# Loads, folds and copies at the head of a linear-attention and GeGLU block, in another order

## The chip, the cores and the metric

The kernel runs on one core of one Trainium2 chip. The metric is the device time of one execution in microseconds (us). A core has TensorE (matrix products, PE in the profile), VectorE (DVE), ScalarE (ACT), GpSimd (POOL) and SyncE (SP, which here issues nearly all transfers), each with its own queue of instructions. They wait for each other by semaphores. PSUM, where products land, is used here as four buffers of two banks each, handed out by a pool.

## The reference

All inputs are bf16. S = 2048 rows, D = 640, 32 heads of 20, F = 1536.

```python
n = layernorm(x)                                 # no scale, no shift
q, k, v = split_heads(n @ wqkv)                  # 32 heads of 20
pq, pk = q @ w_phi[h], k @ w_phi[h]              # 20 x 20 per head
phi(p) = concat(softmax(p), softmax(-p))
kv = einsum("bhsf,bhsd->bhfd", phi(pk), v);  z = sum over s of phi(pk)
o = (phi(pq) @ kv) / (phi(pq) . z + 1e-6)
h = x + o @ wo
out = h + (gelu(layernorm(h) @ w_gate) * (layernorm(h) @ w_up)) @ w_down
```

## The kernel before

The rows are cut into 16 tiles of 128. x lies in four groups of four tiles (`x_sb[0]` to `x_sb[3]`). A tile's LayerNorm is turned by 128 x 128 transposes into `LN1T`, whose five blocks of 128 columns ("chunks" c = 0 to 4) are the left operands of the products with W_v and with W_k. A tile's `v` is ten products of 320 columns (five chunks, two halves), and so is its `k`.

W_k isn't used as it is. It is loaded transposed (`WkT`, five loads d = 0 to 4, line 203) and multiplied with `BD`, a block matrix of w_phi and a mask (lines 430 to 434). That is `fold`: for each d six products into a PSUM buffer `wa`, and then a cast of it into `Wk2` (lines 244 to 259), by VectorE for d = 2 and by ScalarE for the others. `k` products of chunk c need fold c's cast. The exponentials of `k` are made by ScalarE straight from PSUM (line 340).

The order of the work is written out by hand: the kernel's text is the order of each engine's queue. What matters here is the head, lines 187 to 509.

- **Loads** (lines 189 to 205), issued one after another on SP: x tile 0, tile 1, tile 2, W_v chunks 0-1, chunks 2-3, x tile 3, W_v chunk 4, x tiles 4-5, then the five transposing loads of W_k. An x tile or a W_v chunk is 160 KB. x tiles 6-7 come later (line 470). The small w_phi load is on ScalarE's queue. Each load has one of eight semaphores in turn, so the ninth waits for the first to land, and so on.
- **Zero products** (`warm`, lines 225 to 230 and 447): 30 at the start, four more behind the first transposes, all into one PSUM buffer. Their results aren't read.
- **Tiles 0 and 1** (`CT`): VectorE takes off the mean only (`xc`), TensorE transposes (`tr_c`, line 436), ScalarE copies all five chunks in one instruction (line 165). The factor 1/std is put in later, as the scale of `v_ev` (line 316) and of the exponentials.
- **Tile 2, tile 3**: statistics in two halves on VectorE (line 121), the root by two ScalarE instructions (lines 131 and 132), the LayerNorm on VectorE (line 156), transposes on TensorE (line 164), and their copy on VectorE (line 165). In VectorE's queue the copy of tile 2's transposes stands between the two halves of tile 3's statistics, because `between` puts `ln_tp(2, True)` there (line 453).
- **Tiles from 4 on**: transposed by a transfer (line 167) that SP issues when the LayerNorm is written.
- **Products** (lines 448 to 485): `v_part(t, c...)` are tile t's `v` products of these chunks (line 312), `v_mm(t)` all ten (line 296), `v_ev(t)` the copy of `v` out of PSUM on ScalarE, `k_part(t, c...)` tile t's `k` products (line 296).

TensorE's order in the head: the transposes of tiles 0 and 1, four zero products, `v` of tiles 0 and 1 chunks 0-1, tile 0 chunks 2-3, tile 2's transposes, tile 0 chunk 4, tile 1 chunks 2 to 4, `v` of tile 2, tile 3's transposes, folds 0, 1, 2, `v` of tile 3, fold 3, `k` of tile 0 chunks 0 to 2, of tile 1 chunk 0, fold 4, `k` of tile 1 chunks 1-2, of both chunk 3, and in the loop from line 494 on chunk 4 of tile 0, its exponentials, chunk 4 of tile 1, its exponentials, `v` of tile 4, `k` of tile 2, and so on.

The helper of the LayerNorm statistics, which decides VectorE's order through `between`:

```python
for i in range(2):
    nc.vector.bn_stats(stats[:, j, i, :], xt[:, i * HD:(i + 1) * HD])
    if between and i == j == 0:
        between()
```

Of the kernel before, what the change touches and what calls it, by code (L numbers as in the profile page):

```python
# [8 lines left out]
BF16 = mybir.dt.bfloat16  # L9
# [8 lines left out]
def kernel(  # L18
# [12 lines left out]
    nc = tc.nc  # L31
    P = 128
    S = 2048
    D = 640
# [5 lines left out]
    NC = D // P  # L40
# [70 lines left out]
    def gtile(name):  # L111
        return psG.tile([P, 2, 512], F32, name=name, tag="G")
# [46 lines left out]
    def transpose_to(dst, src, on_pe, on_dve=False):  # L159

        if on_pe:
            tp = psG.tile([P, 16, P], BF16, name="tp", tag="G")
            for c in range(NC):
                nc.tensor.transpose(tp[:, c, :], src[:, c * P:(c + 1) * P], ident)  # L164
            (nc.vector.tensor_copy if on_dve else nc.scalar.copy)(dst, tp[:, 0:NC, :])  # L165
        else:
            nc.sync.dma_start_transpose(dst, src)
# [22 lines left out]
    nc.sync.dma_start(x_sb[0][:, 1:2, :], x_v[:, 1:2, :])  # L190
    nc.scalar.dma_start(wphi, phi_v.rearrange("(c p) f -> p c f", p=P))
    nc.scalar.add_instruction(mybir.InstLoadActFuncSet(name=nc.get_next_instruction_name(), act_func_set_id=6))
    nc.sync.dma_start(x_sb[0][:, 2:3, :], x_v[:, 2:3, :])  # L193
    nc.sync.dma_start(Wv[:, 0:2, :], w_v[:, 0:2, 2 * D:3 * D])
    nc.sync.dma_start(Wv[:, 2:4, :], w_v[:, 2:4, 2 * D:3 * D])
    nc.sync.dma_start(x_sb[0][:, 3:4, :], x_v[:, 3:4, :])
    nc.sync.dma_start(Wv[:, 4:5, :], w_v[:, 4:5, 2 * D:3 * D])
    nc.sync.dma_start(x_sb[1][:, 0:2, :], x_v[:, 4:6, :])

    def load_T(WT, i, *ds):  # L200

        for d in ds:
            nc.sync.dma_start_transpose(WT[:, :, d * P:(d + 1) * P], A_wqkv[d * P:(d + 1) * P, i * D:(i + 1) * D])

    load_T(WkT, 1, *range(NC))
    wo_v = A_wo.rearrange("(c p) n -> p c n", p=P)
    wg_v = B_w_gate.rearrange("(c p) n -> p c n", p=P)
# [14 lines left out]
    for i in range(NV):  # L222
        nc.gpsimd.memset(vF[i][:, H * VC:], 1.0)

    wu = gtile("wu")
    def warm(*cols):
        for n in cols:
            nc.tensor.matmul(wu[:, 0, 0:n], lhsT=ones[:, 0:P], rhs=ones[:, 0:n], start=True, stop=True)

    warm(*[512] * 2, *[P] * 28)  # L230

    def fold(WT, W2, quarters, ds=range(NC)):


        n, w = 1, HD
        runs = []
        for c in range(NC):
            lo, hi = H0[c] * Dh, (H0[c] + NH[c]) * Dh
            for r in range(2 * n):
                a, b = max(lo, r * w), min(hi, (r + 1) * w)  # L240
                if a < b:
                    runs.append((r // n, r, c, a, b))
        runs.sort()
        for d in ds:
            wa = gtile("wa")
            wr = wa.rearrange("p u (q x) -> p (u q) x", q=n)
            for i, (u, r, c, a, b) in enumerate(runs):
                nc.tensor.matmul(wr[:, r, a - r * w:b - r * w], lhsT=WT[:, c, d * P:(d + 1) * P],  # L248
                                 rhs=BD[:, c].rearrange("p a b -> p (a b)")[:, a - H0[c] * Dh:b - H0[c] * Dh],
                                 start=(i == 0 or runs[i - 1][0] != u),  # L250
                                 stop=(i + 1 == len(runs) or runs[i + 1][0] != u), skip_group_check=True)
            dst, src = W2[:, d, :].rearrange("p (u f) -> p u f", u=2), wr[:, :, 0:w]
            if quarters:
                dst = W2[:, d, :].rearrange("p (c u m f) -> p u m c f", c=NC, u=2, m=2)
                src = src.rearrange("p u (m c f) -> p u m c f", m=2, c=NC)
            if d in (QA if quarters else KA):
                nc.scalar.copy(dst, src)
            else:
                nc.vector.tensor_copy(dst, src)
# [15 lines left out]
    def ln_st(*tiles, act=True, between=None, log=False):  # L275
        for t, v in zip(tiles, ln_stats(p1, [x_sb[t // 4][:, t % 4, :] for t in tiles], "1", act, between, log)):
            lnp[t] = v

    def ln_ap(t, on_act=False, on_pe=False):
        ln = (ln_act if on_act else ln_dve)(p1, "1", *lnp[t])  # L280
        if on_pe:
            lnp[t] = ln
        else:
            transpose_to(LN1T[t // 4][:, :, t % 4 * P:(t % 4 + 1) * P], ln, False)
# [21 lines left out]
    def v_part(t, *cs):  # L306

        if 0 in cs:
            pv[t] = gtile("pv")
        for c in cs:  # L310
            for u in range(2):
                nc.tensor.matmul(pv[t][:, u, 0:HD], lhsT=lnT(t, c), rhs=Wv[:, c, u * HD:(u + 1) * HD],  # L312
                                 start=(c == 0), stop=(c == NC - 1))

    def v_ev(t):
        nc.scalar.activation(vS[t % NV][:, :, 1:VC].rearrange("p (u h) f -> p u h f", u=2),
                             pv[t][:, :, 0:HD].rearrange("p u (h f) -> p u h f", f=Dh), ACTF.Copy,
                             scale=lnp[t][2] if t in CT else 1.0)
# [7 lines left out]
    def k_part(t, *cs):  # L326
        if 0 in cs:
            pks[t] = gtile("pk")
        proj(pks[t], t, Wk2, cs=cs)
# [100 lines left out]
    def bd(c0, c1):  # L430

        n = c1 - c0
        nc.vector.tensor_tensor(BD[:, c0:c1], wphi[:, c0:c1, None, :].to_broadcast([P, n, 8, Dh]),
                                hmask[:, c0:c1, :, None].to_broadcast([P, n, 8, Dh]), ALU.mult)

    def tr_c(t):
        transpose_to(LN1T[0][:, :, t * P:(t + 1) * P], xc[t], True)

    st_act(1, 0)
    xc = [ln_0(0)]  # L440
    xc.append(xc_a(1))
    tr_c(0)
    tr_c(1)
    ln_st(2, act=False, log=True)
    bd(0, NC)
    st_act(1, 1)
    warm(*[P] * 4)
    v_part(0, 0, 1)
    v_part(1, 0, 1)
    ln_ap(2, on_pe=True)  # L450
    v_part(0, 2, 3)
    root = []
    ln_st(3, act=False, between=lambda: ln_tp(2, True), log=root)
    v_part(0, 4)
    v_ev(0)
    v_part(1, 2, 3)
    root[0]()
    v_part(1, 4)
    v_ev(1)
    v_part(2, *range(NC))  # L460
    d = ident.rearrange("p (r j) -> p r j", r=4)
# [2 lines left out]
    for s, j in ((0, VC + 1), (1, 0)):  # L464
        nc.gpsimd.tensor_scalar(sc[:, s:s + 1], row[:, 0, j:j + 1], -1.0, 1.0, op0=ALU.mult, op1=ALU.add)
        nc.gpsimd.tensor_scalar(bi[:, s:s + 1], row[:, 0, VC:VC + 1], 0.5e-6, row[:, 0, j:j + 1],
                                op0=ALU.mult, op1=ALU.add)
    ln_st(4, act=False, between=lambda: ln_ap(3, on_pe=True))
    ln_tp(3, True)
    nc.sync.dma_start(x_sb[1][:, 2:4, :], x_v[:, 6:8, :])  # L470
    v_ev(2)
    fold(WkT, Wk2, False, (0,))
    fold(WkT, Wk2, False, (1,))
    ln_st(5, act=False, between=lambda: ln_ap(4))
    nc.sync.dma_start(x_sb[2][:, 0:2, :], x_v[:, 8:10, :])
    fold(WkT, Wk2, False, (2,))
    v_mm(3)
    v_ev(3)
    fold(WkT, Wk2, False, (3,))
    k_part(0, 0, 1, 2)  # L480
    k_part(1, 0)
    fold(WkT, Wk2, False, (4,))
    k_part(1, 1, 2)
    k_part(0, 3)
    k_part(1, 3)
    ln_ap(5)
    nc.sync.dma_start(x_sb[2][:, 2:4, :], x_v[:, 10:12, :])
    ln_st(6)
# [5 lines left out]
    for t in range(NT):  # L494
        if t == T3:
            kvp = gtile("kvp")[:, 0, 0:2 * QF].rearrange("p (s f) -> p s f", s=2)
        late = t in (1, 2, 3, 4)
        if 0 < t < NT - 6 and not late:
            ln_ap(t + 6, on_act=True)
        k_tile(t)  # L500
        if t == 0:
            ln_ap(6)
            nc.sync.dma_start(x_sb[3][:, 0:2, :], x_v[:, 12:14, :])
        if t in FQ:
            fold(WqT, Wq2, True, [i for i, f in enumerate(FQ) if f == t])
        for i in KVG.get(t, ()):
            kv_tile(i)
        for j in range(len(QT)):
            if t == QT[j]:
                q_mm(j)  # L510
                q_exp(j)
                if j == 0:
                    nc.gpsimd.tensor_copy(Wg[:, 0, 0:1], Eq[j][:, 0, 1, 0:1])
                for i in KVQ.get(j, ()):
                    kv_tile(i)
        if 0 < t < NT - 3:
            v_mm(t + 3)
        if late:
            ln_ap(t + 6, on_act=True)
        if t == 1:  # L520
            nc.sync.dma_start(x_sb[3][:, 2:4, :], x_v[:, 14:16, :])
        if 0 < t < NT - 3:
            v_ev(t + 3)
        for i in ST.get(t, ()):
            ln_st(i, i + 1)
        k_norm(t)
        load_T(WqT, 0, *[i for i, f in enumerate(LQ) if f == t])
        if t == 10:
            transpose_to(LN1T[0][:, :, P:2 * P], ln_a(1), False)
        if t == 13:  # L530
            ln_ap(0, on_act=True)
        if t == 8:
            for z in KT:
                nc.gpsimd.memset(z, 0.0)
        if t == 5:
            nc.sync.dma_start(Wo, wo_v)
# [401 lines left out]
```

## Time and profile before

| | us |
|---|---|
| median of 3 runs | 271.55 |
| lowest, highest | 271.35, 271.57 |
| the profiled execution | 272.35 |
| its span | 270.6 |
| TensorE busy in it | 266.1 |
| VectorE, ScalarE, GpSimd busy | 173.9, 138.6, 101.2 |

The profile is of one execution. The span goes from its first to its last instruction on the core; the execution's own time holds 1.75 us more around it. A row of the timeline gives start, length, engine, line of the kernel, operation and tiles, how often, and in brackets how long the engine was idle ahead of it and which event ended that. Rows that follow each other with the same operation are merged. The chain of waits is followed back from the last instruction, at each step to what released it. Matmuls overlap, so a row's length is a little more than the time in which the next can start. For transfers the profile gives the issue and the time from issue to landing.

### The profile page before, as it was taken

The numbers are of one execution on the slowest core, as the hardware profiler recorded it, in microseconds if no ns is written. First come the engines' busy times: TensorE is split into PE (matmuls) and PEld (weight loads), VectorE is DVE, ScalarE is ACT, GpSimd is POOL, SyncE is SP. The second block draws the span as 40 slices with busy tenths as digits, with TensorE's granted clock in tenths as the row PEclk, the third lists the DMA queues.
The fourth block names the chain that finished last, engine by engine and source line by source line (L and its number), as shares of the span: only waits on it lengthen the run. The fifth ranks groups of instructions, "written<-read, shape, count | busy, mean of one in ns | idle before, by whom it ended". The sixth has DMA issues, their size and how long they took to land.

```text
span 270.6 us, 7029 instructions
## 1 busy us (share of the span) xinstructions
PE 266.1 (98%) x2857; PEld 172.0 (64%) x2857; DVE 173.9 (64%) x347; ACT 138.6 (51%) x249; POOL 101.2 (37%) x238
## 2 busy tenths in 40 slices
PE   8999999999999999999999999999999999999995
PEld 6777777765455887788755455775555476444574
DVE  5789999996877767876566783568673332333322
ACT  5779997877789675245541356421544300322100
POOL 5448898887002335376211564014661100000000
DMA  6987489213864442432301222203222101000011
GB/s 187 206 199 169 81 210 96 46 37 85 326 201 112 157 101 55 68 78 50 51 27 51 48 50 48 50 3 75 76 46 51 24 24 51 24 0 0 4 48 48
DMA packets 45264, 22.10 MB, mean 82 GB/s; under 512 B 37808, under 2 KB 43184, under 8 KB 45232
## 3 DMA queue, kind: packets, MB, share of 16 engines
q1 hardware_dynamic: 44576, 21.64, 33.5%
q8 instruction: 22, 0.36, 0.6%
q10 hardware_dynamic: 656, 0.03, 0.2%
q14 instruction: 10, 0.08, 0.1%
HBM read 10.18 MB, written 2.62 MB: 47 GB/s over the span
## 4 chain that ended last, share of the span: by engine, by line
PE 96%; DMA 2%; SPq 0%; DVE 0%; issue 0%
PE gu L768 39%; PE pd L790 19%; PE pq L396 8%; PE pk L296 8%; PE po L708 8%; PE pv L296 7%; DMA Wv<-in_A_wqkv_dram 2%; PE kvp L374 2%; PE pv L312 2%; PE ab L619 1%; PE wa L248 1%; PE ab L586 1%; PE tp L164 0%; SPq L193 0%; SPq L190 0%; SPq L189 0%
## 5 line engine op out<-in xcount | busy, mean ns | idle before, releaser
L771 ACT ACTIVATE g<-gu 128x512 bf16<-128x512 f32 (+1 forms) x60 | 30.4, 510 | 74.0 <-PE gu L768 73.2
L774 DVE TENSOR_TENSOR GT<-gu,g 128x512 bf16<-128x512 f32 (+1 forms) x60 | 34.3, 579 | 46.8 <-PE gu L768 38.6
L768 PE MATMUL gu<-LN2T,Wg 128*128 128x512 bf16 (+1 forms) x300 | 61.8, 337 | 0.0
L768 PE MATMUL gu<-LN2T,Wu 128*128 128x512 bf16 (+1 forms) x300 | 61.8, 336 | 0.0
L790 PE MATMUL pd<-Wd,GT 128*128 128x320 bf16 (+4 forms) x396 | 53.9, 295 | 0.0
L790 PEld LDWEIGHTS <-GT 128*128 128x128 bf16 x396 | 37.6, 98 | 14.5 <-DVE GT L774 0.2
L768 PEld LDWEIGHTS <-Wu 128*128 128x128 bf16 x300 | 29.4, 98 | 22.6
L768 PEld LDWEIGHTS <-Wg 128*128 128x128 bf16 x300 | 29.1, 98 | 21.2
L296 PEld LDWEIGHTS <-LN1T 128*128 128x128 bf16 x290 | 28.0, 98 | 10.4
L355 POOL TENSOR_TENSOR E<-E,rs 128x640 bf16<-128x640 bf16 x25 | 31.7, 1295 | 4.4 <-DVE rs L351 2.8
L792 DVE TENSOR_TENSOR y<-pd,x_sb 128x320 bf16<-128x320 f32 (+4 forms) x33 | 15.8, 480 | 24.1 <-PE pd L790 24.1
L708 PE MATMUL po<-Wo,oT 128*128 128x320 bf16 x160 | 24.5, 299 | 0.0
L296 PE MATMUL pk<-Wk,LN1T 128*128 128x320 bf16 x160 | 24.4, 299 | 0.0
L396 PE MATMUL pq<-LN1T,Wq 128*128 128x512 bf16 x100 | 22.9, 379 | 0.0
L347 DVE TENSOR_REDUCE sk<-E 128x64 f32<-128x1280 bf16 x16 | 22.9, 1430 | 0.0
L401 ACT ACTIVATE Eq<-pq 128x1024 bf16<-128x1024 f32 (+1 forms) x26 | 19.9, 831 | 2.8 <-PE pq L396 2.7
L340 ACT ACTIVATE E<-pk 128x640 bf16<-128x640 f32 x28 | 19.1, 769 | 3.0 <-PE pk L296 3.0
L708 PEld LDWEIGHTS <-oT 128*128 128x128 bf16 x160 | 15.6, 98 | 7.3 <-ACT oT L165 0.2
L296 PE MATMUL pv<-Wv,LN1T 128*128 128x320 bf16 x130 | 19.8, 299 | 0.0
L151 ACT ACTIVATE ln<-x_sb,v,rstd 128x640 bf16<-128x640 bf16 x14 | 12.9, 920 | 13.0 <-POOL v L747 12.9
L396 PEld LDWEIGHTS <-Wq 128*128 128x128 bf16 x100 | 9.4, 98 | 10.3
L683 DVE TENSOR_TENSOR tt<-AB,w 128x1280 bf16<-128x1280 f32 x10 | 15.1, 1505 | 0.4 <-POOL w L676 0.3
(120 smaller groups left out, 291.4 us busy)
## 6 DMA issues: line engine op xcount, KB each, us to landing
out_dram<-y SPq DMA_DIRECT2D x15, 160.0 KB, 1.8
x_sb<-in_A_x_dram SPq DMA_DIRECT2D x6, 320.0 KB, 3.3
Wd<-in_B_w_down_dram SPq DMA_DIRECT2D x1, 1440.0 KB, 6.8
Wg<-in_B_w_gate_dram SPq DMA_DIRECT2D x1, 1152.0 KB, 7.3
Wu<-in_B_w_up_dram SPq DMA_DIRECT2D x1, 1152.0 KB, 5.6
Wo<-in_A_wo_dram SPq DMA_DIRECT2D x1, 800.0 KB, 5.0
Wg<-in_B_w_gate_dram SPq DMA_DIRECT2D x1, 768.0 KB
Wu<-in_B_w_up_dram SPq DMA_DIRECT2D x1, 768.0 KB, 9.1
```

What stands on the lines that cost most here:

```text
L296: nc.tensor.matmul(ps[:, u, 0:HD], lhsT=lnT(t, c), rhs=W[:, c, u * HD:(u + 1) * HD], start=(c == 0), stop=(c == NC - 1))
L340: nc.scalar.activation(Ek[t][:, s, :].rearrange("p (u f) -> p u f", u=2), pk[:, :, 0:HD], ACTF.Exp, scale=((lnp[t][2], nrstd[t]) if t in C ...
L347: nc.vector.reduce_sum(sk, Ek[t].rearrange("p s (h f) -> p (s h) f", f=Dh), axis=AX.X)
L355: eng.tensor_tensor(e, e, rs[:, s * H:(s + 1) * H, None].to_broadcast([P, H, Dh]), ALU.mult)
L396: nc.tensor.matmul(pqs[j][:, i, :], lhsT=Wq2[:, kc, c * P:(c + 1) * P], rhs=LN1T[b][:, kc, :], start=(kc == 0), stop=(kc == NC - 1))
L401: nc.scalar.activation(Eq[j][:, :, s, :], pqs[j][:, 0:len(QG[j])], ACTF.Exp, scale=(1.0, -1.0)[s])
L708: nc.tensor.matmul(pos[u], lhsT=st[t][:, c, :], rhs=Wo[:, c, u * HD:(u + 1) * HD], start=(c == 0), stop=(c == NC - 1))
L768: nc.tensor.matmul(gu[i][:, 0:n], lhsT=W[:, c, f * P:(f + 1) * P], rhs=LN2T[b][:, c, a0:a1], start=(c == 0), stop=(c == NC - 1))
L771: nc.scalar.activation(g[:, 0:n], gu[0][:, 0:n], ACTF.Gelu_apprx_tanh)
L774: nc.vector.tensor_tensor(st[b, "g", f][:, a0:a1], gu[1][:, 0:n], g[:, 0:n], ALU.mult)
L790: nc.tensor.matmul(pd[:, 0:f1 - f0], lhsT=st[b, "g", f][:, tl * P:(tl + 1) * P], rhs=Wd[:, f, f0:f1], start=(f == 0), stop=(f == NF - 1), ...
L792: nc.vector.tensor_tensor(y[:, f0:f1], pd[:, 0:f1 - f0], x_sb[b][:, tl, f0:f1], ALU.add)
```

## The change

The loads: W_v's chunk 0 becomes the third transfer, ahead of x tile 2; the other chunks go in pairs 1-2 and 3-4; x tiles 6-7 are issued ahead of the five W_k loads. Behind SP's x tiles 4-5 nothing else changes place.

The zero products: the first goes into a PSUM buffer of its own, the others into a second one. The four behind the transposes stay where they are in TensorE's order.

Tiles 0 and 1: the copy of the transposes is cut in two pieces, chunks 0-1 and chunks 2 to 4, in the order tile 0, tile 1, tile 0, tile 1. The mask matrix `BD` is made in two pieces, chunks 0-1 ahead of tile 2's statistics and the rest behind them.

TensorE's order becomes: transposes of tiles 0 and 1, four zero products, chunk 0 of tiles 0 and 1, chunks 1-2 of tiles 0 and 1, chunks 3-4 of tile 0, tile 2's transposes, chunks 3-4 of tile 1, `v` of tile 2, fold 0, tile 3's transposes, fold 1, `v` of tile 3, folds 2 and 3, `k` chunk 0 of tiles 0 and 1, fold 4, `k` chunks 1 to 4 of tile 0, its exponentials, `k` chunks 1 to 4 of tile 1, its exponentials, `v` of tile 4. With the pool's order of buffers fold 4 now takes the one that fold 2 leaves, the products `v` of tile 3 the one that fold 0 leaves, and `k` of tile 1 the one of `v` of tile 3.

```diff
+    nc.sync.dma_start(Wv[:, 0:1, :], w_v[:, 0:1, 2 * D:3 * D])
     nc.sync.dma_start(x_sb[0][:, 2:3, :], x_v[:, 2:3, :])
-    nc.sync.dma_start(Wv[:, 0:2, :], w_v[:, 0:2, 2 * D:3 * D])
-    nc.sync.dma_start(Wv[:, 2:4, :], w_v[:, 2:4, 2 * D:3 * D])
+    nc.sync.dma_start(Wv[:, 1:3, :], w_v[:, 1:3, 2 * D:3 * D])
+    nc.sync.dma_start(Wv[:, 3:5, :], w_v[:, 3:5, 2 * D:3 * D])
     nc.sync.dma_start(x_sb[0][:, 3:4, :], x_v[:, 3:4, :])
-    nc.sync.dma_start(Wv[:, 4:5, :], w_v[:, 4:5, 2 * D:3 * D])
     nc.sync.dma_start(x_sb[1][:, 0:2, :], x_v[:, 4:6, :])
...
+    nc.sync.dma_start(x_sb[1][:, 2:4, :], x_v[:, 6:8, :])
     load_T(WkT, 1, *range(NC))
...
-    wu = gtile("wu")
-    def warm(*cols):
+    def warm(wu, *cols):
...
-    warm(*[512] * 2, *[P] * 28)
+    warm(gtile("wu"), 512)
+    wu = gtile("wu")
+    warm(wu, 512, *[P] * 28)
...
+    tpc = []
     def tr_c(t):
-        transpose_to(LN1T[0][:, :, t * P:(t + 1) * P], xc[t], True)
+        tpc.append(psG.tile([P, 16, P], BF16, name="tp", tag="G"))
+        for c in range(NC):
+            nc.tensor.transpose(tpc[t][:, c, :], xc[t][:, c * P:(c + 1) * P], ident)
+    def cp_c(t, a, b):
+        nc.scalar.copy(LN1T[0][:, a:b, t * P:(t + 1) * P], tpc[t][:, a:b, :])
...
     tr_c(0)
     tr_c(1)
+    warm(wu, *[P] * 4)
+    for a, b in ((0, 2), (2, NC)):
+        for t in CT:
+            cp_c(t, a, b)
+    bd(0, 2)
     ln_st(2, act=False, log=True)
-    bd(0, NC)
+    bd(2, NC)
     st_act(1, 1)
-    warm(*[P] * 4)
-    v_part(0, 0, 1)
-    v_part(1, 0, 1)
+    v_part(0, 0)
+    v_part(1, 0)
+    v_part(0, 1, 2)
+    v_part(1, 1, 2)
     ln_ap(2, on_pe=True)
-    v_part(0, 2, 3)
+    v_part(0, 3, 4)
     root = []
     ln_st(3, act=False, between=lambda: ln_tp(2, True), log=root)
-    v_part(0, 4)
     v_ev(0)
-    v_part(1, 2, 3)
+    v_part(1, 3, 4)
     root[0]()
-    v_part(1, 4)
     v_ev(1)
     v_part(2, *range(NC))
...
+    fold(WkT, Wk2, False, (0,))
     ln_st(4, act=False, between=lambda: ln_ap(3, on_pe=True))
     ln_tp(3, True)
-    nc.sync.dma_start(x_sb[1][:, 2:4, :], x_v[:, 6:8, :])
     v_ev(2)
-    fold(WkT, Wk2, False, (0,))
     fold(WkT, Wk2, False, (1,))
     ln_st(5, act=False, between=lambda: ln_ap(4))
     nc.sync.dma_start(x_sb[2][:, 0:2, :], x_v[:, 8:10, :])
-    fold(WkT, Wk2, False, (2,))
     v_mm(3)
     v_ev(3)
+    fold(WkT, Wk2, False, (2,))
     fold(WkT, Wk2, False, (3,))
-    k_part(0, 0, 1, 2)
+    k_part(0, 0)
     k_part(1, 0)
     fold(WkT, Wk2, False, (4,))
-    k_part(1, 1, 2)
-    k_part(0, 3)
-    k_part(1, 3)
+    k_part(0, 1, 2, 3)
     ln_ap(5)
...
         k_tile(t)
         if t == 0:
+            k_part(1, 1, 2, 3)
             ln_ap(6)
```

## The prediction

> **What bounds the kernel now.** I read first the page's busy shares, then the chain that ended last in order of time, then the timeline of the first 18 us, because the change touches nothing later.
>
> ```profile
> span 270.6 us, 7029 instructions
> PE 266.1 (98%) x2857; PEld 172.0 (64%) x2857; DVE 173.9 (64%) x347; ACT 138.6 (51%) x249; POOL 101.2 (37%) x238
> ```
>
> ```profile
> 2.18 5.18 DMA Wv<-in_A_wqkv_dram
> 7.41 1.79 PE pv L312 x12
> 9.20 0.28 PE tp L164 x5
> 9.47 2.44 PE pv L312 x18
> ...
> 12.20 0.98 PE wa L248 x18
> 13.19 1.36 PE pv L296 x10
> ```
>
> From 7.41 us on the chain is TensorE, piece upon piece without a hole. Ahead of it stands one transfer, the first 320 KB of W_v. So the time is 7.41 us, plus a fixed amount of TensorE work, plus the tail. The change adds no product and takes none away. It can win only by starting TensorE's dense stretch earlier, and whatever hole it tears into that stretch is lost in full. The row of 18 products gives the pitch: 2.44 / 18 = 0.1356 us for one of 320 columns. Five transposes take 0.28 us, one fold (6 `wa` products) 0.98 / 3 = 0.33 us.
>
> The timeline shows how tight the stretch is (columns: start, length, what, and in brackets the idle time before it and who ended it):
>
> ```profile
> 4.88 1.25 PE L164 MATMUL tp<-ident,xc 128*128 128x128 bf16 x10
> 5.57 0.89 DVE L121 BATCH_NORM_STATS2 stats<-x_sb 128x6 f32<-128x320 bf16 x2 [0.32 <-DMA x_sb<-in_A_x_dram]
> 5.63 1.29 ACT L165 COPY LN1T<-tp 128x640 bf16<-128x640 bf16 x2 [0.37 <-PE tp L164]
> 5.92 0.63 PE L228 MATMUL wu<-const-bfloat16-1.0 128*128 128x128 bf16 x4
> 7.41 1.79 PE L312 MATMUL pv<-Wv,LN1T 128*128 128x320 bf16 x12 [0.85 <-DMA Wv<-in_A_wqkv_dram]
> 7.48 0.44 DVE L156 TENSOR_SCALAR ln<-x_sb,mv,rstd 128x640 bf16<-128x640 bf16 x1
> 8.61 0.49 DVE L121 BATCH_NORM_STATS2 stats<-x_sb 128x6 f32<-128x320 bf16 x1 [0.68 <-DMA x_sb<-in_A_x_dram]
> 9.03 0.44 PE L164 MATMUL tp<-ident,ln 128*128 128x128 bf16 x5
> 9.51 0.49 DVE L165 COPY LN1T<-tp 128x640 bf16<-128x640 bf16 x1 [0.41 <-PE tp L164]
> 11.25 0.45 DVE L156 TENSOR_SCALAR ln<-x_sb,mv,rstd 128x640 bf16<-128x640 bf16 x1 [0.24 <-ACT rstd L132]
> 11.76 0.45 PE L164 MATMUL tp<-ident,ln 128*128 128x128 bf16 x5
> 12.26 0.48 DVE L165 COPY LN1T<-tp 128x640 bf16<-128x640 bf16 x1
> 13.02 1.52 PE L296 MATMUL pv<-Wv,LN1T 128*128 128x320 bf16 x10
> 14.35 0.77 DVE L259 CAST Wk<-wa 128x640 bf16<-128x640 f32 x1
> 14.58 0.70 ACT L316 ACTIVATE vS<-pv 128x640 bf16<-128x640 f32 x1 [0.74 <-PE pv L296]
> 15.78 0.48 PE L248 MATMUL wa<-BD,WkT 128*128 128x140 bf16 x6
> 16.30 0.69 ACT L257 CAST Wk<-wa 128x640 bf16<-128x640 f32 x1 [0.43 <-PE wa L248]
> 17.73 1.52 PE L296 MATMUL pv<-Wv,LN1T 128*128 128x320 bf16 x10
> ```
>
> Two clocks run side by side. One is TensorE's work. The other is x tile 3: its transposes (11.76) stand right behind its LayerNorm (11.25 + 0.45 = 11.70). That LayerNorm hangs on VectorE, which must first copy tile 2's transposes (9.51), since that copy stands between the two halves of tile 3's statistics. So TensorE's products of tile 3 already wait, nearly, for another engine than the first W_v chunk.
>
> **The change part by part.** *The first chunk.* It takes x tile 2's place as the third transfer, with the same 160 KB. Tile 2 landed at about 5.55 (VectorE was released at 5.57), so the chunk does. The first piece of tile 0's copy starts at 5.63 as now. For 256 of 640 columns it takes between 0.28 (in proportion) and 0.64 us (half of 1.29); I take 0.4, near proportion. TensorE's four zero products end at 5.92 + 0.63 = 6.55 and stand ahead in its order. Their pitch is 0.107 (the ten transposes and they go from 4.88 on), so the first real product can be issued at about 6.4 instead of 7.41: a lead of 1.0 us.
>
> *The second chunk.* Only four products hang on chunk 0 (tiles 0 and 1, two halves each). Then tile 0 needs chunks 1 and 2, which are the fifth transfer. In units of 160 KB, what had landed when:
>
> ```profile
> L194 SPq DMA_DIRECT2D Wv<-in_A_wqkv_dram x1: 433/433/433, 2.2 to 2.2; - x1
> L195 SPq DMA_DIRECT2D Wv<-in_A_wqkv_dram x1: 469/469/469, 2.7 to 2.7; - x1
> ...
> DMA to landing us min/median/max: 5.2/5.3/5.5
> ```
>
> Three units at 5.55; five at 7.36 (2.18 + 5.18 in the chain); seven at about 8.17 (2.66 + 5.5); eight at about 8.6 (tile 3, from its row at 8.61). In the new order tile 2 is the fourth unit (about 6.45), chunks 1-2 end at the sixth: between 7.36 and 8.17, so **7.77**. Chunks 3-4 end at the eighth (8.6), tile 3 at the ninth (9.0, 0.4 later than now). TensorE goes on at 7.77 + 0.04 = 7.81.
>
> *On to tile 3.* Twelve products stand ahead of tile 2's transposes: 7.81 + 12 x 0.1356 = 9.44 (now 9.03). Tile 2's LayerNorm is there: 7.48 + 0.44 now, 0.9 later for its later landing, 8.8; the mask's second piece, which stands ahead of it on VectorE, is shorter than the whole mask that stands there now. From the transposes to the copy is 9.51 - 9.03 = 0.48, so the copy starts at 9.92. Tile 3's own path would allow 9.0 + 0.43. From that copy to tile 3's transposes is 11.76 - 9.51 = 2.25 now: 9.92 + 2.25 = 12.17. From those transposes to the end of their copy is 12.26 + 0.48 - 11.76 = 0.98, and 0.05 on to the product: products of tile 3 at **13.20**, against 13.02 now: 0.18 later. The lead of 1.0 us has turned into idle TensorE: 0.86 us ahead of chunk 1 (four products from 6.4 are done at 6.95), 0.2 ahead of tile 2's products (9.92 + 0.49 + 0.05 = 10.46, wanted at 9.44 + 0.28 + 4 x 0.1356 = 10.26), and 0.4 between fold 1 (ended at 12.17 + 0.28 + 0.33 = 12.78) and tile 3's.
>
> *The folds.* Now folds 0, 1 and 2 (0.98) lie between tile 3's transposes and its products and cover the copy. In the new order only fold 1 does; fold 0 goes ahead of the transposes, where TensorE would wait anyway, and fold 2 behind the products. So behind 13.20 stands 0.33 us more work than now behind 13.02.
>
> *Buffers and k of tile 0 first.* Fold 4 takes the buffer that fold 2 leaves, and fold 2 is now emptied by VectorE late. Fold 2 starts at 13.20 + 1.36 = 14.56; a fold's cast can start 16.30 - 15.78 = 0.52 later and takes 0.77: free at 15.89. TensorE reaches fold 4 after folds 2, 3 and four `pk` products: 14.56 + 0.66 + 0.54 = 15.76. A wait of 0.13. Then ScalarE's cast of fold 4 (0.52 + 0.69) ends at 17.10, but only six `pk` products stand between (15.89 + 0.33 + 0.81 = 17.03), where now eight on two tiles do: a wait of 0.07. The second `pk` buffer waits for tile 3's `v`: 13.20 + (14.58 - 13.02) + 0.70 = 15.46, just when it is wanted. Together 0.2; bounds 0 (VectorE and ScalarE free, casts in proportion) and 0.5. That ScalarE's exponentials of tile 0 come earlier is worth nothing: TensorE has no hole behind them to close.
>
> *x tiles 6 and 7 ahead of W_k.* One more issue ahead of the five transposing loads, 0.43 to 0.58 us on SP's queue, and 320 KB ahead of them on the wire.
>
> ```profile
> 4.63 7.69 SPq L203 DMA_TRANSPOSE WkT<-in_A_wqkv_dram  x5
> 12.36 0.58 SPq L470 DMA_DIRECT2D x_sb<-in_A_x_dram  x1
> ```
>
> ```profile
> DMA to landing us min/median/max: 3.5/4.5/5.9
> ```
>
> The fifth load is issued at about 11.0 now and lands between 11.0 + 3.5 and 11.0 + 4.5; fold 4 wants it at 15.78. Afterwards it is issued about 0.5 later, and nothing is issued right behind it, so I take 3.5 to 4: 15.0 to 15.5, ahead of 15.89, no cost. With 4.5 and the 320 KB added (two units, 0.8) it is 16.8: 0.9 lost. What leaves the place at 12.36 frees SP for nothing: its next transfer, tile 4's transpose, waits for VectorE.
>
> *At nothing:* the zero products in two banks (same count; the buffer of tile 1 waits for the last of them, which ends at 6.55); the mask in two (one more VectorE start, at most 0.2 us, beside the wait for tile 2); two more copies on ScalarE (at most 0.2 us each, its next work waits for tile 2's statistics, which come later). If tile 2 came early, those 0.4 us would stand ahead of its LayerNorm, still 0.1 us ahead of need.
>
> *The sum:* 0.18 (products of tile 3) + 0.33 (fold 2 behind them) + 0.2 (two waits) = **0.7 us later** than now at the first product of tile 4 (17.73 now), from where everything is as before. The profiled execution took 272.35 us (span 270.6 and 1.75 around it): 273.05. It stands 0.8 above the median of the runs, 271.55, whose like is then **272.25 us**.
>
> [...] In the trace four products of 128 columns took 0.63 us at 5.92 and five took 0.44 us at 9.03: the array still ran at half pace at 6.55 and no longer at 7.41. [...] The row bears on the first four products at 6.4, which then cost 0.27 each; the forecast hides that in the wait for chunk 1.
>
> **The rivals.** *Chunks 1-2 land early (not slower).* Three units came at 5.55 and five at 7.36: 0.9 a unit, against 0.4 a unit afterwards, so the five may have been held up by something that won't recur. At 0.4 a unit from 5.55, six land at 6.75. Then TensorE runs through: 6.4 + 4 x 0.1356 = 6.95 for chunk 1 (7.5 at half pace), 0.86 (0.3) earlier than forecast, and tile 3's chain with it as long as tile 3 lands by 8.6. Time: 0.7 - 0.86 = -0.16 to 0.7 - 0.3 = +0.4, so 271.4 to 271.95. It decides from a landing before 7.4. For it: the 0.4 a unit later on; against it: the 5.18 us of the chain row.
>
> *The fifth W_k load is late.* Fold 4 waits for it until 16.3 to 16.8 in place of 15.89: +0.4 to +0.9 on top of the forecast, 272.65 to 273.15. For it: it landed close to fold 4 already; against: x tiles 6, 7 no longer stand behind it.
>
> [...]
>
> *The lead survives.* For a gain over 0.54 us all of tile 3's chain must move up by 1.25 us against the forecast; the zero products alone hold the start at 6.4, so I see no such path, and leave it a small chance for what I don't see.
>
> **How the numbers follow.** Forecast (chunks 1-2 at 7.4 to 8.2, so +0.35 to +1.15): 0.51. Early chunks: 0.24. Late W_k: 0.14. Half pace: 0.05. A gain over 0.2%: 0.06. The bound of 0.2% is 0.54 us, about what a measurement of this kernel tells from no change. Slower by more: 0.43 of the forecast, late W_k and half pace, 0.62. Within: early chunks and 0.08 of the forecast, 0.32. Faster 0.06. The range goes from the early chunks (271.4) to late W_k (273.1).
>
> **What would show it.** Right: the first `pv` product near 6.4, then a hole ahead of the fifth; tile 2's copy near 9.9; tile 3's products no earlier than 13.0 with a hole ahead of them; the first product of tile 4 at 18.2 to 18.6 (17.73 now). Wrong: chunks 1-2 landed before 7, no hole between fold 1 and tile 3's products, or any hole in TensorE behind 18.6.

## The result and the profile after

| | median us | lowest to highest | executions |
|---|---|---|---|
| before | 271.5 | 271.23 to 271.57 | 6 |
| after | 273.1 | 272.74 to 273.38 | 6 |

The ratio is 1.0053, 95% interval 1.0038 to 1.0068: slower by 1.6 us, where 0.7 was forecast. The profiled execution of the changed kernel took 272.74 us.

The first rows of its page (span; busy time of the engines): TensorE is as busy as before, 265.5 against 266.1 us, and the span is 0.4 us longer.

```profile
span 271.0 us, 7016 instructions
...
PE 265.5 (98%) x2841; PEld 171.2 (63%) x2857; DVE 174.1 (64%) x348; ACT 139.0 (51%) x251; POOL 101.7 (38%) x238
```

The chain of waits of the changed kernel, first 19 us (start, length, what; SPq is SyncE's queue of transfers). Before, one landing of W_v stood ahead of TensorE's dense stretch, at 7.41. Now the chain begins with SP's issues one behind the other, runs through the issue of the third W_k load, which holds SP for 2.00 us, and ends in the fourth load's landing at 9.82 + 4.83 = 14.65. Only then does TensorE's unbroken part begin.

```profile
5.11 1.30 SPq L203
...
6.46 1.27 SPq L203
...
7.78 2.00 SPq L203
...
9.82 4.83 DMA WkT<-in_A_wqkv_dram
```

TensorE's timeline of the changed kernel:

```profile
6.01 2.50 PE L314 MATMUL pv<-Wv,LN1T 128*128 128x320 bf16 x16
8.34 0.44 PE L164 MATMUL tp<-ident,ln 128*128 128x128 bf16 x5
8.62 2.28 PE L314 MATMUL pv<-Wv,LN1T 128*128 128x320 bf16 x14
10.81 0.49 PE L250 MATMUL wa<-BD,WkT 128*128 128x140 bf16 x6
11.14 0.44 PE L164 MATMUL tp<-ident,ln 128*128 128x128 bf16 x5
11.42 0.48 PE L250 MATMUL wa<-BD,WkT 128*128 128x140 bf16 x6
12.17 1.53 PE L298 MATMUL pv<-Wv,LN1T 128*128 128x320 bf16 x10 [0.27 <-DVE LN1T L165]
13.54 0.48 PE L250 MATMUL wa<-BD,WkT 128*128 128x140 bf16 x6
14.70 0.49 PE L250 MATMUL wa<-BD,WkT 128*128 128x140 bf16 x6 [0.69 <-DMA WkT<-in_A_wqkv_dram]
15.03 0.71 PE L298 MATMUL pk<-Wk,LN1T 128*128 128x320 bf16 x4
15.57 0.48 PE L250 MATMUL wa<-BD,WkT 128*128 128x140 bf16 x6
15.88 2.46 PE L298 MATMUL pk<-Wk,LN1T 128*128 128x320 bf16 x16
18.18 1.11 PE L298 MATMUL pv<-Wv,LN1T 128*128 128x320 bf16 x7
```

From the first `pv` product (6.01) to the first of tile 4 (18.18) it is 12.17 us. With the prediction's pitch (0.1356 a product, 0.28 five transposes, 0.33 a fold) the holes are: 8.34 - 6.01 - 16 x 0.1356 = 0.16 among the first 16 products; 10.81 - 8.62 - 14 x 0.1356 = 0.29 around tile 2's products (0.21 ahead of them, 0.08 behind them ahead of fold 0); 12.17 - 11.42 - 0.33 = 0.42 ahead of tile 3's; 14.70 - 13.54 - 0.33 = 0.83 ahead of fold 3; about 0.1 in `k` of tile 0. That is 1.8 in all. The differences between kernels arise nearly all ahead of tile 4: what an execution takes beyond the first `pv` product of tile 4 is 254.5 to 255.1 us in every profile of this case but one (named below).

### The profile page after: what moved, and what is told of

Read it like the earlier page. It is cut to its first block, busy times and chain, and to the rows that moved or that the text cites. A ratio compares the mean times of both kernels' runs of the same rounds, so it can differ in the third digit from the quotient of the medians.

```text
span 271.0 us, 7016 instructions
## 1 busy us (share of the span) xinstructions
PE 265.5 (98%) x2841; PEld 171.2 (63%) x2857; DVE 174.1 (64%) x348; ACT 139.0 (51%) x251; POOL 101.7 (38%) x238
## 3 DMA queue, kind: packets, MB, share of 16 engines
HBM read 10.18 MB, written 2.62 MB: 47 GB/s over the span
## 4 chain that ended last, share of the span: by engine, by line
PE 93%; SPq 3%; DMA 2%; issue 1%; DVE 0%
PE gu L779 38%; PE pd L801 19%; PE pk L298 8%; PE po L719 8%; PE pq L398 8%; PE pv L298 6%; DMA WkT<-in_A_wqkv_dram 2%; PE kvp L376 2%; SPq L203 2%; PE ab L630 1%; PE ab L597 1%; PE wa L250 1%; PE tp L164 0%; SPq L196 0%; SPq L197 0%
## 5 line engine op out<-in xcount | busy, mean ns | idle before, releaser
L342 ACT ACTIVATE E<-pk 128x640 bf16<-128x640 f32 x28 | 18.5, 730 | 2.9 <-PE pk L298 2.9
L151 ACT ACTIVATE ln<-x_sb,v,rstd 128x640 bf16<-128x640 bf16 x14 | 12.9, 920 | 13.0 <-POOL v L758 12.9
```

What stands on the lines that cost most here:

```text
L342: nc.scalar.activation(Ek[t][:, s, :].rearrange("p (u f) -> p u f", u=2), pk[:, :, 0:HD], ACTF.Exp, scale=((lnp[t][2], nrstd[t]) if t in C ...
```

## The experiments

Three theories stood against each other. O: the order of folds and products costs the time, as the prediction said. W: W_k's loads come late because x tiles 6 and 7 stand ahead of them. F, a finer W: a transfer of TensorE's own instructions holds up the W_k load that is in flight. C, later: with x tiles 6 and 7 ahead, other landings come late. Times are medians, measured in three series with the kernel before run beside each: it took 271.83 us in the first series (the first four kernels below) and 271.63 in the other two. A "+" is the distance from it.

| kernel | median us | ratio, 95% interval |
|---|---|---|
| before_again | 271.67 | 0.9996 [0.9986, 1.0005] |
| head_alone | 272.09 | 1.001 [1.0001, 1.002] |
| x67_back | 272.63 | 1.0026 [1.0016, 1.0035] |
| after_w0 | 273.0 | 1.0041 [1.0025, 1.0058] |
| folds_alone | 272.21 | 1.0024 [1.0014, 1.0033] |
| before_x67 | 272.74 | 1.0043 [1.0032, 1.0055] |
| after_wide | 272.88 | 1.0047 [1.003, 1.0064] |
| head_wide | 272.19 | 1.0024 [1.0011, 1.0037] |
| before_x67_w0 | 271.76 | 1.0013 [1.0001, 1.0026] |
| after_again | 273.03 | 1.0052 [1.0039, 1.0066] |
| after_w0_again | 272.66 | 1.0037 [1.0023, 1.0051] |
| after_early | 274.7 | 1.0115 [1.0101, 1.0129] |

**The kernel before, once more (before_again; no edit).**

> The kernel before, unchanged, profiled a second time. Its first profiled execution (272.35 us) is 0.85 above its median (271.5), the changed kernel's (272.74) 0.36 below its own (273.1). If the first profile of before caught a rare late landing of W_v chunks 0-1 (7.36 us), this one starts its first product between 6.4 and 6.6 and takes about 271.5. If the profile alone adds the time, it starts at 7.4 again and takes 272.3.

Profiled at 271.52, near the median. Its chain and its timeline of TensorE:

```profile
2.18 4.22 DMA Wv<-in_A_wqkv_dram
```

```profile
6.44 1.79 PE L312 MATMUL pv<-Wv,LN1T 128*128 128x320 bf16 x12 [0.33 <-DMA Wv<-in_A_wqkv_dram]
8.07 0.44 PE L164 MATMUL tp<-ident,ln 128*128 128x128 bf16 x5
...
10.79 0.44 PE L164 MATMUL tp<-ident,ln 128*128 128x128 bf16 x5
11.07 1.15 PE L248 MATMUL wa<-BD,WkT 128*128 128x140 bf16 x18
12.06 1.52 PE L296 MATMUL pv<-Wv,LN1T 128*128 128x320 bf16 x10
...
16.82 1.52 PE L296 MATMUL pv<-Wv,LN1T 128*128 128x320 bf16 x10
```

W_v's first load landed after 4.22 us, not 5.18. The execution profiled first was 0.85 above the median, and this one landing accounts for it: the first product came 7.41 - 6.44 = 0.97 later. The three other profiles of kernels with this order of W_v loads start it at 6.22 to 6.45, so the early landing is the usual one. From 6.44 on there is no hole up to tile 4 (10.38 us). Against this profile tile 4 comes 18.18 - 16.82 = 1.36 later in the changed kernel: the 1.8 us of holes less 0.43 of earlier start (1.42 in the changed kernel's second profile, after_again).

**The first part alone (head_alone).** W_v's first chunk early, copies in pieces, zero products in two banks; folds and x tiles 6, 7 as before.

```diff
+    nc.sync.dma_start(Wv[:, 0:1, :], w_v[:, 0:1, 2 * D:3 * D])
     nc.sync.dma_start(x_sb[0][:, 2:3, :], x_v[:, 2:3, :])
...
+    for a, b in ((0, 2), (2, NC)):
+        for t in CT:
+            cp_c(t, a, b)
```

> Only the first part of the change on the kernel before: W_v's chunk 0 third, pairs 1-2 and 3-4, copies and mask in pieces, zero products in two buffers, and the products of tiles 0 and 1 in the new order. x tiles 6, 7, the folds and the k products stand as before. Theory W: the loss is all in the second part, so this is 270.9 to 271.6. Theory O, in which the lead at the start is turned into a wait for tile 3: 271.4 to 271.8. If the first part itself is at fault: over 272.

+0.26 us, barely clear of no change. In absolute time that is above the ranges of both theories and just over the third one's 272; but the kernel before had taken 271.5 when they were written, and it stood 0.3 higher here. Measured from it, 0.26 lies in O's range (-0.1 to +0.3). Either way this part gains nothing even by itself. Its timeline of TensorE:

```profile
5.88 2.52 PE L313 MATMUL pv<-Wv,LN1T 128*128 128x320 bf16 x16
8.23 0.44 PE L164 MATMUL tp<-ident,ln 128*128 128x128 bf16 x5
...
10.95 0.45 PE L164 MATMUL tp<-ident,ln 128*128 128x128 bf16 x5 [0.15 <-DVE ln L156]
```

TensorE starts 0.56 earlier, and yet tile 2's transposes come at 8.23 instead of 8.07, because 16 products stand ahead of them and not 12: 4 x 0.1356 = 0.54, just the lead, and small holes among the 16 add 8.23 - 5.88 - 16 x 0.1356 = 0.18. Tile 2's copy, and behind it tile 3's LayerNorm, hang on those transposes, so tile 3 comes 10.95 - 10.79 = 0.16 later, and TensorE waits there for that LayerNorm.

**The folds alone (folds_alone).** The kernel before with only the new order of folds and of `k`.

```diff
+    fold(WkT, Wk2, False, (0,))
     ln_st(4, act=False, between=lambda: ln_ap(3, on_pe=True))
...
-    fold(WkT, Wk2, False, (2,))
     v_mm(3)
     v_ev(3)
+    fold(WkT, Wk2, False, (2,))
...
-    k_part(0, 0, 1, 2)
+    k_part(0, 0)
```

> The kernel before, and only the new order of folds and of k (fold 0 ahead of tile 3's transposes, fold 2 behind tile 3's v, k of tile 0 first); loads, copies and zero products as before. Theory O: fold 2's 0.33 us behind tile 3's v and the two waits of 0.2 make 272.2 to 272.5 where before is 271.8. Theory F: the fourth load lands ahead of the instruction transfer as before, so nothing is waited for but what the order itself costs; if tile 3's path has slack for fold 0 and 2's change of place, 271.7 to 272.1.

+0.58 us: O's range, at its lower end in absolute time. In its timeline the row with the wait is the one ahead of tile 3's products:

```profile
11.23 0.48 PE L248 MATMUL wa<-BD,WkT 128*128 128x140 bf16 x6
11.98 1.53 PE L296 MATMUL pv<-Wv,LN1T 128*128 128x320 bf16 x10 [0.27 <-DVE LN1T L165]
...
17.35 1.52 PE L296 MATMUL pv<-Wv,LN1T 128*128 128x320 bf16 x10
```

One fold between tile 3's transposes and its products doesn't cover the copy. From tile 3's products to tile 4's it is 17.35 - 11.98 = 5.37 against 16.82 - 12.06 = 4.76: 0.61 more, of which fold 2 is 0.33 and waits 0.28. The prediction had 0.33 + 0.2.

**Everything but x tiles 6 and 7 (x67_back).** The changed kernel with that load issued where it was before.

```diff
-    nc.sync.dma_start(x_sb[1][:, 2:4, :], x_v[:, 6:8, :])
     load_T(WkT, 1, *range(NC))
...
     ln_tp(3, True)
+    nc.sync.dma_start(x_sb[1][:, 2:4, :], x_v[:, 6:8, :])
```

> The changed kernel with x tiles 6 and 7 issued where they were, behind tile 3's transposes; all else as changed. Theory W (the W_k loads, put behind 320 KB more, land late and fold 3 or 4 waits): the hole of 0.8 us ahead of fold 3 goes, 272.0 to 272.4. Theory O (the new order of folds, products and copies costs the time, whatever the loads do): 272.9 to 273.2, and fold 3 or fold 4 still waits or the holes lie elsewhere.

+0.80. In absolute time it lies between the two ranges; but the kernel before stood 0.3 higher here than when they were written, and with that added 272.63 lies in W's (272.3 to 272.7). The hole ahead of fold 3 is gone, since folds 2 and 3 run as one row of 12 products:

```profile
13.72 0.79 PE L249 MATMUL wa<-BD,WkT 128*128 128x140 bf16 x12
```

What remains agrees with the sum of the last two kernels, 0.26 + 0.58 = 0.84, each of them sure to about 0.25 us. In the changed kernel 0.6 to 0.8 more (273.03 - 271.63 or 273.1 - 271.5, less 0.80) are left to x tiles 6 and 7.

**x tiles 6 and 7 alone (before_x67),** the opposite edit on the kernel before.

> The kernel before, and only x tiles 6 and 7 issued ahead of the five W_k loads. Theory F: in every profile so far one 16 KB transfer of TensorE's instructions, at 12.6 to 13.3 us, holds up the W_k load that is then in flight by about 1.5 us; before, that is the fifth load, with the two x tiles ahead it is the fourth (14.65 us in the changed kernel), which fold 3 wants at about 13.9. In this kernel fold 3 stands behind tile 3's v and is wanted at 14.3 (first profile) or 13.4 (the usual execution), so its wait should be 0.3 to 1.2: 272.4 to 273.1 where before is 271.8. Theory O (the order of folds and products costs the time, the loads nothing): 271.6 to 272.0.

+1.11: the largest of the parts, and O falls for this one. Its timeline of TensorE, then its chain:

```profile
11.37 1.07 PE L249 MATMUL wa<-BD,WkT 128*128 128x140 bf16 x12
12.88 0.49 PE L249 MATMUL wa<-BD,WkT 128*128 128x140 bf16 x6 [0.45 <-DMA WkT<-in_A_wqkv_dram]
13.21 1.52 PE L297 MATMUL pv<-Wv,LN1T 128*128 128x320 bf16 x10
15.13 0.49 PE L249 MATMUL wa<-BD,WkT 128*128 128x140 bf16 x6 [0.41 <-DMA WkT<-in_A_wqkv_dram]
```

```profile
7.76 2.57 SPq L203
...
10.37 4.72 DMA WkT<-in_A_wqkv_dram
```

Not only fold 3 waits. Folds 0 to 2, which stand ahead of tile 3's products in this order, wait as well: tile 3's products come at 13.21 instead of 12.06, and that 1.15 I had not expected. Fold 3 adds 15.13 - 13.21 - 1.36 = 0.56. Tile 4 comes 18.49 - 16.82 = 1.67 later in this profile; its execution (272.98) is the slowest of five, so the median holds less of both waits.

**The same with folds that need only the first load (before_x67_w0).** Folds 0 to 4 all read the first W_k load, so folds 1 to 4 compute another's values.

```diff
-                nc.tensor.matmul(wr[:, r, a - r * w:b - r * w], lhsT=WT[:, c, d * P:(d + 1) * P],
+                nc.tensor.matmul(wr[:, r, a - r * w:b - r * w], lhsT=WT[:, c, (d * P if quarters else 0):(d * P + P if quarters else P)],
```

> The kernel before with x tiles 6 and 7 ahead of the W_k loads, and folds 0 to 4 all reading the first W_k load (so folds 1 to 4 wait for no later load and their values are another's; W_q's folds as ever). x tiles 6, 7 ahead alone took 272.74 with before at 271.63. Theory W: the 1.1 us is fold 3's wait for the fourth W_k load, 271.5 to 271.9 here. Theory C: x tiles 6, 7 cost by something else (other landings, SP's queue), 272.5 to 272.9 here.

271.76: of the 1.11 us 0.98 are gone, with the same transfers in the same order. So nearly all of that cost is the folds' wait for the later W_k loads, and not something else that x tiles 6 and 7 do. C falls for the kernel before.

**The changed kernel once more (after_again), and with that edit (after_w0, after_w0_again).**

> The changed kernel, unchanged, beside the others of this call. It took 273.1 with before at 271.5. Both theories: 272.8 to 273.3, its profile again with a hole ahead of fold 3.

> The changed kernel, but every fold reads the first of the five W_k loads, so the folded W_k is not the reference's; the four other loads run as they did and no product waits for them. Theory W: 271.9 to 272.3, with no hole at the folds. Theory O: 272.8 to 273.1. What it takes above the kernel before is what the order costs without any wait for W_k.

> The changed kernel with folds 0 to 4 reading the first W_k load (folds 1 to 4 hold another's values), timed beside the changed kernel itself. It took 273.0 the first time, with x tile 3 late in its profile. Theory W (fold 3's wait is 0.5 to 0.8 of the time): 0.4 to 0.8 below the changed kernel of this call, 272.2 to 272.6. Theory C (late W_v and x tile 3 landings make most of it): within 0.3 of it, 272.7 to 273.1.

The first trial, 273.0, came out in O's range; its profiled execution took 273.28, and I put that down to a late landing of x tile 3. None of its folds reads the later W_k loads. Beside the changed kernel itself it is 273.03 against 272.66: 0.37 less, 0.03 short of W's range. The two series of executions overlap by 0.3 us (272.49 to 273.53, and 272.21 to 272.79), so this size is less sure than the 0.98. The profile of after_again bears it out, since folds 2 and 3 wait less in it than in the changed kernel's first profile: their row and the next one's start (15.08) leave 15.08 - 14.13 - 2 x 0.33 = 0.29 for the fourth load.

```profile
14.13 1.11 PE L250 MATMUL wa<-BD,WkT 128*128 128x140 bf16 x12
```

Another wait is larger there. Weight loads of TensorE:

```profile
11.40 0.31 PEld L250 LDWEIGHTS <-WkT 128*128 128x128 bf16 x6 [0.63 <-DMA WkT<-in_A_wqkv_dram]
```

This is fold 0, waiting for the *first* load. (The row of its products names a copy of ScalarE that ended at the same time; in the other profile fold 0 starts at 10.81 while that copy runs from 10.43 for 0.78 us, so it is not what fold 0 needs.) In the new order fold 0 stands ahead of tile 3's transposes, so this wait moves tile 3: its products come at 12.76 here and at 12.17 in the other profile, and 11.41 - 8.83 against 10.81 - 8.62, that is 0.39 of the 0.59, arises ahead of fold 0. The experiment can't take it out, since the first load is still needed; it may be part of what remains. That is argued, not shown.

**Which load is late: wide and narrow zero products.** In every profile one transfer of 16 KB of instructions starts at 11.8 to 14.3 us, and one W_k load or the transfer behind it lands late about then. To move it without moving the loads, I changed how many instructions stand ahead: in after_wide and head_wide 7 zero products of 512 columns replace 28 of 128, in after_early 56 of 64 do.

```diff
-    warm(wu, 512, *[P] * 28)
+    warm(wu, 512, *[512] * 7)
```

> The changed kernel with its 28 zero products of 128 columns replaced by 7 of 512: the same time on TensorE, 21 instructions fewer ahead of everything. Theory F: the transfer of instructions is set off by TensorE's place in its program, so it comes 21 products (2 to 3 us) later, the fourth W_k load lands at about 13.1 instead of 14.65, the 0.84 us hole ahead of fold 3 goes, and the time falls by 0.5 to 0.9 to 272.2 to 272.6. Theory O, or a hold-up by the queue of loads itself: the fourth load stays at 14.5 or later and the time at 273.0 to 273.3.

> The first part alone (W_v chunk 0 early, copies in pieces, two banks) on the kernel before, which took 272.09 with before at 271.83, and the same 7 wide zero products. Theory F: the fifth load, at 15.0 in the first part alone and just gating fold 4 there, lands at about 13.5, so fold 4 waits for nothing: 271.6 to 272.0, 0.1 to 0.5 less than the first part alone. Theory O: nothing changes, 272.0 to 272.2.

> The changed kernel with 56 zero products of 64 columns in place of 28 of 128: 28 instructions more ahead of everything, about the same time. Theory F: the transfer of TensorE's instructions comes earlier, at 10 to 11 us in place of 12.8, and holds up the first or second W_k load (fold 0 or 1 late by up to 1 us), while the fourth lands at 13 to 13.5 with no hole ahead of fold 3; time 272.6 to 273.4. If the hold-up hangs on the queue of loads and not on that transfer, the fourth load lands at 14.5 or later again.

The page of transfers for 0.2 us (queue, packets, MB, share of 16 engines) shows the instruction transfer of the changed kernel in the window 12.7 to 12.9; 29.2% of 16 x 0.2 us is one engine for 0.93 us:

```profile
q8 instruction: 1, 0.02, 29.2%
```

and that of after_wide in the window 13.9 to 14.1 (it took 1.17 us):

```profile
q8 instruction: 1, 0.02, 36.5%
```

It moved by over a microsecond, and the late load moved with it. The chain of after_wide:

```profile
10.16 1.28 SPq L203
...
11.48 4.78 DMA WkT<-in_A_wqkv_dram
```

The fourth load, issued from 10.16, no longer ends anybody's wait: folds 2 and 3 stand in one row without a hole,

```profile
13.94 0.79 PE L250 MATMUL wa<-BD,WkT 128*128 128x140 bf16 x12
...
16.31 0.49 PE L250 MATMUL wa<-BD,WkT 128*128 128x140 bf16 x6 [0.98 <-DMA WkT<-in_A_wqkv_dram]
```

but the fifth takes 4.78 and fold 4 waits for it in turn. So the hole moved by one fold and did not close. The time decides nothing: the median, 272.88 against the changed kernel's 273.03, is above F's range, but the seven executions go from 272.22 to 273.99, three of them are in that range, and the profiled one is the slowest. In head_wide F's time failed: 272.19, +0.56, where head_alone was +0.26 (the intervals overlap). The fifth load did land earlier there, at 13.37 by the trace instead of 15.02, but fold 4 had waited for it for under 0.1 us.

In after_early the packet starts at 11.8, not at 10 to 11 as expected. Some 1.2 us after its start hardly any packet begins, as in the changed kernel. Half-microsecond windows, of after_early and then of the changed kernel; the first column behind the comma is TensorE's busy time, the last two are the packets' share of the engines' time and their GB/s, and they book a packet wholly in the window where it starts:

```profile
13.00:13.50 0.50, 0.43 (x4) 0.32 (x5) 0.42 (x2) 0.50 (x2) 0.48 (x1) 1.00 0.08 9
```

```profile
13.00:13.50 0.50, 0.50 (x6) 0.39 (x4) 0.50 (x2) 0.22 (x1) 0.00 (x0) 1.00 1.93 150
13.50:14.00 0.50, 0.50 (x8) 0.29 (x5) 0.21 (x1) 0.27 (x1) 0.17 (x1) 1.00 1.32 41
14.00:14.50 0.50, 0.01 (x1) 0.00 (x0) 0.45 (x1) 0.44 (x1) 0.42 (x2) 1.00 0.08 10
```

In the last row TensorE stands still as well (0.01 of 0.50 us). The engines are not free there: by the trace, 19 packets of 256 bytes that began between 13.2 and 13.9 took 0.68 to 1.27 us each, and they are what is in flight. So little data moves, and yet the engines are held.

The fourth load of after_early was no earlier (its chain has 10.37 + 4.73 = 15.10), so that expectation failed. It is the third that is late there: by the trace it took 5.91 us and landed at 13.93, where it took 4.46 in the changed kernel. The 274.7 us have two other sources besides: W_v's second load landed late, and in `k` at 58 us there is a hole that nothing in the profile releases:

```profile
7.69 1.79 PE L314 MATMUL pv<-Wv,LN1T 128*128 128x320 bf16 x12 [1.00 <-DMA Wv<-in_A_wqkv_dram]
```

```profile
58.18 0.30 PE L298 MATMUL pk<-Wk,LN1T 128*128 128x320 bf16 x1 [1.02 <-issue]
```

This is the one kernel that takes longer beyond tile 4 than the others, 255.8 us.

The same kind of hold-up occurs without an instruction packet. Windows of the kernel before, first profile, where the pages of transfers for 7 to 10.5 us list no such packet:

```profile
8.50:9.00 0.50, 0.50 (x6) 0.38 (x4) 0.39 (x1) 0.00 (x0) 0.49 (x1) 1.00 2.39 122
9.00:9.50 0.50, 0.50 (x9) 0.43 (x7) 0.10 (x1) 0.00 (x0) 0.41 (x3) 1.00 0.06 26
```

Its first W_k load took 5.93 us, against 4.91 in before_again.

F stands as follows. By the traces, the fourth load took 3.5 to 3.9 us in the seven profiles in which it had landed by the packet's start (or within 0.1 us of it), and 4.3 to 4.8 in the six in which it was then in flight. All six have x tiles 6 and 7 ahead; what tells the packet from those tiles is after_wide, with the same loads, a packet 1.2 us later and 3.86 us for the fourth load, and after_early, where the late load is the third. So the late load follows the packet when the number of instructions ahead is changed. By the traces the 16 KB are one packet, which takes 0.93 to 1.30 us of one engine. How it costs a transposing load that much isn't shown, and a load can be held up without it.

## Why the prediction was right and wrong

**Right: no gain from the early first chunk, and slower.** The lead doesn't reach tile 3, as the prediction said. Its reason was a landing, though; head_alone's timeline shows that four more products ahead of tile 2's transposes are enough. Of its own signs the first product came earlier than forecast (6.01, not 6.4), the hole ahead of the fifth was missing, and tile 3's products came at 12.17 and not at 13.0 or later; tile 4's 18.18 is within 0.02 of the forecast 18.2 to 18.6 by other holes.

**Right, and nearly in size: the folds.** 0.33 for fold 2 and 0.2 for waits were forecast from tile 3's products on; 0.33 and 0.28 were measured. The hole of 0.4 ahead of tile 3's products is there (0.42).

**Wrong: "chunks 1-2 ... between 7.36 and 8.17, so 7.77".** That step was interpolated in the execution whose first W_v load was late. Sixteen products ran from 6.01 to 8.34 with 0.16 us of holes, so chunks 1-2 were never waited for by more than that, and the forecast hole of 0.86 ahead of the fifth product isn't there. By the traces they landed at 6.23 to 7.07 in eight of the nine profiles with the new order of W_v loads. The ninth is after_early, 7.65, with a hole of 1.00; a smaller one is in x67_back, where they landed at 6.91:

```profile
6.95 1.79 PE L313 MATMUL pv<-Wv,LN1T 128*128 128x320 bf16 x12 [0.24 <-DMA Wv<-in_A_wqkv_dram]
```

Tile 2's copy started at 8.82 here and 9.03 in after_again, not 9.92. This is the rival "chunks 1-2 land early", but without its price, for the next reason.

**Wrong: the lead of 1.0 us, and the step from 272.35 to the median.** The prediction took 0.8 off at the end, because the profiled execution stood that much above the median, and counted a lead of 1.0 from the same execution. Both were one thing: 0.97 us of that W_v landing. In a usual execution the start moves from 6.44 to 6.01 or 5.89, a lead of 0.43 to 0.55. The forecast's holes amounted to (18.4 - 6.4) - (17.73 - 7.41) = 1.7 between the first product and tile 4, the measured ones to 1.8; it is the lead that was counted too large, by half a microsecond, and that nearly is the difference between the forecast 0.7 and 1.36.

**Wrong: "x tiles 6 and 7 ahead of W_k ... no cost".** That the holes come out alike in sum, and the time within the range, is luck: in place of 0.86 for chunk 1 there is 0.83 for the fourth W_k load. The prediction looked at the fifth load and fold 4 alone. What was late is what is needed earlier: the fourth load for fold 3 (0.83 in one profile of the changed kernel, 0.29 in the other), and the first for fold 0 (0.08 and 0.47). Two causes add up for the fourth, which lands at 14.65 against 12.60 in before_again. It is issued 9.82 - 8.70 = 1.12 later by the traces: the issue of the third load holds SP for 2.0 to 2.8 us, where it is 1.3 to 1.8 in the kernels without x tiles 6 and 7 ahead, on top of the 0.48 for one more issue. And it takes 4.83 instead of 3.90, being now the one in flight at the instruction packet. Before, the fifth is the late one: 14.82 by the trace in before_again, just ahead of fold 4 at 14.87. Alone it costs 1.11, of which 0.98 is the wait for W_k; in the whole change 0.6 to 0.8; that it is less there because fold 2 is wanted later, behind tile 3's products, is argued.

**The half pace** (0.05 of the chances) didn't stay: the four zero products took less, not more, than the 0.63 before. That holes ahead of 8 us keep TensorE at it, no run shows; behind the hole of 1.00 us in after_early twelve products of 320 columns took 1.79 us, as they did behind one of 0.33 in before_again.

```profile
5.66 0.39 PE L228 MATMUL wu<-const-bfloat16-1.0 128*128 128x128 bf16 x4
```

**A slip in the sum.** Fold 2's buffer, by the terms given, is free at 14.56 + 0.52 + 0.77 = 15.85, not 15.89, so that wait is 0.09 and not 0.13. It changes nothing above.

The sum, then: 0.26 for the first part, 0.58 for the folds and `k` first, the rest up to 1.4 to 1.6 for x tiles 6 and 7. The predicted sign was right; the time is 0.85 us above the predicted one and at the range's upper end.

## What to carry to other kernels

Where the profiled execution stands off the median, find the row in which it does before you count a gain from that row: a change that removes a wait can't gain what the usual execution doesn't lose there. A head start is worth something only if it reaches the chain that sets the next start, so count the instructions ahead of that chain's first link; here four more products ate nearly all of it (0.54 of 0.56 us). A load moved ahead of a series can delay each member of it (here the first was issued 5.11 - 4.63 = 0.48 us later, the fourth 1.12), so check each member against its own first use, not the last one against the last.

## What the runs showed of the hardware

- The landing of the same first W_v load varied from 4.22 to 5.18 us between two executions of one kernel, and that accounts for an execution 0.85 us above the median.
- The page of transfers counts instructions beside the data, as a share of the same 16 engines: one 16 KB packet, 0.93 to 1.30 us, at 11.8 to 14.3 us here. Its place followed the number of TensorE's instructions ahead (12.8 in the changed kernel, 11.8 with 28 more of them, 14.0 with 21 fewer), and the transposing load that was then in flight landed late: the fourth 4.3 to 4.8 us after its issue, against 3.5 to 3.9 where it was down by then; the fifth of head_wide, down ahead of the packet, took 13.37 - 10.18 = 3.2, and head_alone's 4.9. That the packet is the cause is argued.
- The windows' share and GB/s book a packet where it starts (1.93 and 1.32 of the engines' time in two windows), so a window with next to none (0.08) can be full of long ones: 19 packets of 256 bytes took 0.68 to 1.27 us in the changed kernel.
- TensorE left its slower pace at different times in executions of like kernels: four products of 128 columns took 0.39 us at 5.66 in the changed kernel, and in the kernel before 0.63 us at 5.92 in one execution and 0.39 at 5.72 in the other. What sets that time isn't shown.
- Issuing a transposing load mostly took SP 1.26 to 1.30 us, but the third of the series 2.0 to 2.8 us when one more load stood ahead of it. In all fourteen profiles the third's issue ended 0.14 to 0.23 us ahead of the landing of the last x load in front of the series (9.78 and 9.94 in the changed kernel, 8.66 and 8.88 in before_again). So it goes with that landing, which is about 1 us later with x tiles 6 and 7 ahead; why the third and no other waits for it is open.
